# Zeros, x and conversions moved in the opening of a three-layer kernel

## The chip, the cores and the metric

The kernel runs on one core of one Trainium2 chip. Its time is device microseconds (us) of one execution; the kernel before takes 930.06 us (median of 3 runs, 930.0 to 930.53). One execution was also recorded by the profiler: it took 930.29 us, of which 928.4 us lie between its first and its last instruction (the span). In the rows, PE is TensorE, PEld its weight loads, DVE VectorE, ACT ScalarE, POOL GpSimd and SP SyncE, whose queue issues most DMAs.

## The reference

```python
def mab(q, kv):                                   # one attention, scale = 1/sqrt(128)
    s = scale * (q @ kv.transpose(0, 2, 1))
    s = s - s.max(-1, keepdims=True)
    a = np.exp(s)
    a /= a.sum(-1, keepdims=True) + 1e-09
    return a @ kv
h = mab(I, x)                                     # x: 12480 x 128, I: 32 x 128
x = mab(x, h)                                     # 12480 x 128
h = x @ w_in                                      # 128 -> 2048
x = (np.maximum(h, 0) + alpha * np.minimum(h, 0)) @ w_out
h = np.maximum(x @ w2_in, 0)                      # 128 -> 2048
out = (h * h) @ w2_out
```

x and I are 32-bit floats, the four weight matrices 64-bit floats.

## The kernel before, in words

**Opening.** The first attention (32 queries over all 12480 rows of x) goes over seven groups: group 0 has 4 tiles of 48 rows, groups 1 to 6 have 4 tiles of 512. For each group PE transposes x (`transpose_x`, L290), DVE and ACT copy the result into `xT` (L293), PE makes the scores (L302), DVE their running maximum (L318 to L322), ACT the exponentials (L331) and the factor for older sums (L326), PE transposes those (`transpose_e`, L346), ACT copies them (L352), and PE multiplies them with x (`values1`, L360); DVE adds the result into `h_run` (L367). The values of a group are taken in the turn of the next. Loops are in the order written; a tile's readers and writers wait by semaphore, and every engine and every DMA queue works strictly in its order.

**Keeping PE at work.** Ahead of the first x, and between short pieces, PE multiplies a tile of zeros into a bank that nobody reads (`keep_busy`, L97).

**Conversions.** The weights arrive as pairs of 32-bit words (`load_w`, 512 KB a piece, four buffers). A piece is made into 32-bit floats in five steps (`to_f32`): MAG (ACT, L196), LOW (ACT, L199), BITS (DVE, L203), SIGN (DVE, L209), ADD (POOL, L212). `convs[0..3]` are the pieces of w_in, `convs[4..7]` those of w_out, which have three steps more: REST (POOL, L227, times 1 - alpha), HI (ACT, L232, the rounded part) and LO (POOL, L217, what is left). They stand between the attention's steps, where the code puts them. A raw buffer is free for the next load once its ADD is done.

**From the first attention to the layers.** The normalized result is `hT` (L486). From it PE makes the scores of the first tile of 512 rows (L513), `w1h` and `w1l` (hT times w_in, split in two), whose rows SP's DMAs spread into `w1s` (L650). PIECES are the eight pieces of the second MLP's weights.

**Main loop.** Step s does four parts of the MLPs for 128 of 2048 columns of one tile of rows: `l1_a(s)` (one matmul, L729, then ACT L735 and DVE L742 split it in `g1h` and `g1l`), `l1_b` of an earlier step (three matmuls with `wo_hi` and `wo_lo`, L747 to L749), and the same for the second MLP from step 24 on (7 matmuls more). 25 tiles of 16 chunks make 400 steps. Before step 24 `l1_a` writes four banks in turn, so that `l1_a(s)` waits until DVE has read the bank of step s - 4; `l1_b(i)` comes at step i + 5. Work that comes once is put at a step by `at(step, ...)`: it follows that step's matmuls. At step 12 `step_v` (L701) multiplies all 16 chunks of `w_out_sb` in 16 small matmuls, chunk by chunk.

```python
    at(8, scale_wa)
    at(8, second[6])
    at(12, step_v)
```

## Time and profile before

| What | Value |
|---|---|
| Median of 3 runs | 930.06 us |
| The profiled execution | 930.29 us |
| Its span | 928.4 us |
| PE busy | 921.3 us (99%) |
| DVE, ACT, POOL busy | 644.2, 728.7, 535.7 us |
| First x transposed on PE, from | 3.28 us |
| `hT` written, from | 38.06 us |
| First matmul of step 0 | 43.58 us |

The profile tells one execution. The chain of waits is followed back from the last instruction: it names at each moment the engine for which the end waited. The timeline gives instructions in order of time, merged where neighbours are alike; a row's second number runs from the start of the first to the end of the last, so matmuls that overlap are read by the distance of their starts. A matmul of 32-bit floats counts twice in these rows.

### The profile page before, as it was taken

The page shows a single profiled execution, that of the slowest core. Times are in us where ns is not written, and L with a number is a line of the kernel's source. Part 1 is how long each engine was busy: PE and PEld are TensorE (multiplying, and loading weights), DVE is VectorE, ACT ScalarE, POOL GpSimd, SP SyncE. Part 2 cuts the span into 40 slices and gives each one's busy share as a digit, 9 for nine tenths or more (in the row PEclk, how much of TensorE's full clock was granted, in tenths as well). Part 3 has the DMA queues.
Part 4 walks back from the last instruction along what each step waited for, and adds up shares of the span by engine and source line. Part 5 has one row for each costly group of instructions (what it writes and reads, how often), then busy time and mean ns, then how long its engine had stood idle before and what let it go on. Part 6 is the DMA issues. An engine that isn't in the chain of part 4 may idle for free.

```text
span 928.4 us, 13643 instructions
## 1 busy us (share of the span) xinstructions
PE 921.3 (99%) x4549; PEld 784.2 (84%) x4549; DVE 644.2 (69%) x1014; ACT 728.7 (78%) x1336; POOL 535.7 (58%) x436
## 2 busy tenths in 40 slices
PE   9999999999999999999999999999999999999998
PEld 7677888888888888888888888888888888899997
DVE  5898776666666766667766666766666766666677
ACT  6889877777777787777787777877777877878776
POOL 2568755655555665555665555665555565655530
PEclk9999999999999999999999999999999999999999
DMA  9551000010000020000020000020000010000000
GB/s 344 179 151 47 7 7 12 21 37 12 1 12 12 1 57 13 1 12 13 1 57 12 1 12 7 7 57 2 12 12 1 12 36 15 12 12 11 1 11 19
DMA packets 64551, 29.00 MB, mean 31 GB/s; under 512 B 52208, under 2 KB 57440, under 8 KB 64480
## 3 DMA queue, kind: packets, MB, share of 16 engines
q1 hardware_dynamic: 64000, 27.52, 12.0%
q8 instruction: 36, 0.59, 0.3%
q10 hardware_dynamic: 480, 0.61, 0.2%
q14 instruction: 35, 0.29, 0.1%
HBM read 14.80 MB, written 6.39 MB: 23 GB/s over the span
## 4 chain that ended last, share of the span: by engine, by line
PE 93%; DVE 1%; ACT 1%; DMA 0%; issue 0%; SPq 0%; ACTq 0%
PE y L749 18%; PE y L747 18%; PE y L748 18%; PE h L747 9%; PE h L749 9%; PE h L748 9%; PE h L729 9%; DVE g1l L742 1%; PE y L765 1%; PE ms L570 1%; DVE mag L209 0%; ACT g1h L735 0%; DMA w1s<-w1h 0%; PE h L728 0%; PE y L701 0%
## 5 line engine op out<-in xcount | busy, mean ns | idle before, releaser
L792 POOL TENSOR_TENSOR g2l<-sq,g2h 128x512 fp32r<-128x512 f32 (+1 forms) x376 | 477.0, 1269 | 320.1 <-ACT g2h L790 277.4
L742 DVE SCALAR_TENSOR_TENSOR g1l<-h,g1h 128x512 fp32r<-128x512 f32 (+2 forms) x399 | 269.0, 676 | 215.8 <-ACT g1h L735 213.2
L735 ACT ACTIVATE g1h<-h 128x512 fp32r<-128x512 f32 (+2 forms) x400 | 234.1, 588 | 123.6 <-PE h L729 120.8
L783 DVE TENSOR_TENSOR sq<-h,r 128x512 f32<-128x512 f32 (+2 forms) x400 | 271.1, 678 | 44.0 <-ACT r L781 13.7
L781 ACT ACTIVATE r<-h 128x512 f32<-128x512 f32 (+2 forms) x400 | 235.2, 588 | 54.0 <-PE h L749 14.3
L790 ACT CAST g2h<-sq 128x512 fp32r<-128x512 f32 (+2 forms) x400 | 240.9, 602 | 0.4 <-DVE sq L783 0.3
L729 PE MATMUL h<-a_s,w1s 128*128 128x512 f32 (+3 forms) x400 | 151.1, 379 | 1.2 <-DVE g1l L742 0.7
L747 PE MATMUL h<-y1h,w2i_hi 128*128 128x512 f32 (+2 forms) x400 | 151.1, 378 | 0.4 <-DVE sq L783 0.2
L749 PE MATMUL y<-g2l,w2o_hi 128*128 128x512 f32 (+2 forms) x400 | 150.8, 377 | 0.0
L747 PE MATMUL y<-g1h,wo_hi 128*128 128x512 f32 (+2 forms) x400 | 150.6, 377 | 0.0
L749 PE MATMUL h<-y1l,w2i_hi 128*128 128x512 f32 (+2 forms) x400 | 150.6, 377 | 0.0
L749 PE MATMUL y<-g1l,wo_hi 128*128 128x512 f32 (+2 forms) x400 | 150.6, 377 | 0.0
L747 PE MATMUL y<-g2h,w2o_hi 128*128 128x512 f32 (+2 forms) x400 | 150.6, 377 | 0.0
L748 PE MATMUL y<-g2h,w2o_lo 128*128 128x512 f32 (+2 forms) x400 | 150.6, 376 | 0.0
L748 PE MATMUL h<-y1h,w2i_lo 128*128 128x512 f32 (+2 forms) x400 | 150.6, 376 | 0.0
L748 PE MATMUL y<-g1h,wo_lo 128*128 128x512 f32 (+2 forms) x400 | 150.5, 376 | 0.0
L729 PEld LDWEIGHTS h<-a_s,w1s 128*128 128x128 f32 (+1 forms) x400 | 74.9, 187 | 16.4 <-DVE g1l L742 3.0
L747 PEld LDWEIGHTS h<-y1h,w2i_hi 128*128 128x128 f32 x400 | 74.9, 187 | 13.7 <-DVE g1l L742 1.0
L748 PEld LDWEIGHTS y<-g1h,wo_lo 128*128 128x128 f32 x400 | 75.0, 187 | 12.3
L747 PEld LDWEIGHTS y<-g1h,wo_hi 128*128 128x128 f32 x400 | 75.0, 187 | 11.9
L749 PEld LDWEIGHTS y<-g2l,w2o_hi 128*128 128x128 f32 x400 | 74.9, 187 | 11.9 <-DVE g2l L792 0.2
L749 PEld LDWEIGHTS h<-y1l,w2i_hi 128*128 128x128 f32 x400 | 74.9, 187 | 11.5
(160 smaller groups left out, 659.6 us busy)
## 6 DMA issues: line engine op xcount, KB each, us to landing
out_dram<-o SPq DMA_DIRECT2D x84, 64.0 KB, 2.0
xg<-in_x_dram SPq DMA_DIRECT2D x8, 512.0 KB, 9.5
raw<-in_moe_w_in_dram SPq DMA_DIRECT2D x8, 512.0 KB, 5.7
raw<-in_moe_w_out_dram SPq DMA_DIRECT2D x8, 512.0 KB, 5.0
a_s<-a_hi SPq DMA_DIRECT2D x40, 64.0 KB, 2.0
a_s<-a_lo SPq DMA_DIRECT2D x40, 64.0 KB, 2.0
x_last<-in_x_dram SPq DMA_DIRECT2D x2, 512.0 KB, 9.6
out_dram<-o SPq DMA_DIRECT2D x12, 56.0 KB, 1.9
```

Of the source, the lines that this page charges most:

```text
L570: nc.tensor.matmul(b[i * M : (i + 1) * M, :w], hT[:, :M], xT[:, first_token[t + 1] - w : first_token[t + 1]], start=True, stop=True, tile_ ...
L729: nc.tensor.matmul(eights(b[:, :w]), w1s[: a.shape[0], c * P : (c + 1) * P], eights(a), start=True, stop=True)
L735: nc.scalar.activation(hi, b[:, :w], AF.Relu)
L742: nc.vector.scalar_tensor_tensor(lo, b[:, :w], 0.0, f32(hi), op0=ALU.max, op1=ALU.subtract)
L747: nc.tensor.matmul(b, w_hi, hi, start=start, stop=False)
L748: nc.tensor.matmul(b, w_lo, hi, start=False, stop=False)
L749: nc.tensor.matmul(b, w_hi, lo, start=False, stop=stop)
L765: nc.tensor.matmul(eights(b), v_s[: a.shape[0]], eights(a), start=False, stop=True)
L781: nc.scalar.activation(r, b, AF.Relu)
L783: nc.vector.tensor_tensor(sq, b, r, op=ALU.mult)
L790: nc.scalar.copy(hi, sq)
L792: (nc.vector if i >= total - LAG2 else nc.gpsimd).tensor_tensor(lo, sq, f32(hi), op=ALU.subtract)
```

## The change

Five zero matmuls stand at the beginning in place of four, and the transposition of the inducing rows (`indT`) comes right behind them, ahead of the first x. In the loop over groups, the values of the group before are no longer behind the scores but between the transposition of the next x and the next scores, half on either side of `transpose_e`; the ACT copy of a group's first tile stands ahead of its exponentials. BITS, SIGN and ADD of a piece of w_in come one group after its MAG and LOW. The pieces of w_out follow by one place each: where `convs[5]` and `convs[6]` were handled, `convs[4]` and `convs[5]` are, and the end of `convs[6]` and all of `convs[7]` but its load stand in steps 4 to 13 of the main loop. x of groups 2 and 3 is loaded whole ahead of the piece of w_in beside it, x of group 6 ahead of the first w_out, and PIECES[2] and PIECES[3] are loaded at steps 5 and 10.

```diff
--- before.py
+++ after.py
@@ -96,7 +96,7 @@
         for _ in range(n):
             nc.tensor.matmul(b[:, :P], v, v, start=True, stop=True)
 
-    keep_busy(4, idle_bank)
+    keep_busy(5, idle_bank)
 
 
 
@@ -234,7 +234,7 @@
         def low():
             pool_lo(lo, a, hi)
 
-        return to_f32("w_out", k, lambda: f, h2_bank if k == 2 else None) + [rest, high, low]
+        return to_f32("w_out", k, lambda: f, h2_bank if k == 1 else None) + [rest, high, low]
 
     def conv_w2(name, k, tags, bank):
         f = []
@@ -266,12 +266,10 @@
     al_raw = st.tile([NCH, P], F32, name="al_raw", tag="al_raw")
     load_x(0)
     load_x(1)
-    load_x(2, 0)
+    load_x(2)
     load_w("w_in", 0)
-    load_x(2, 1)
-    load_x(3, 0)
+    load_x(3)
     load_w("w_in", 1)
-    load_x(3, 1)
     nc.sync.dma_start(out=al_raw, in_=alpha.rearrange("(c p) -> c p", p=P))
     load_x(4)
     load_w("w_in", 2)
@@ -373,48 +371,52 @@
             v()
 
     convs = [conv_w_in(k) for k in range(4)] + [conv_w_out(k) for k in range(4)]
-    evac = transpose_x(0)
-    run(evac)
+    MAG, LOW, BITS, SIGN, ADD, REST, HI, LO = range(8)
+
     indT = keep_tile("indT", [P, M])
     b = free_bank()
     nc.tensor.transpose(b[:, :M], ind, ident[:M, :M])
     nc.vector.tensor_copy(indT, b[:, :M])
+    evac = transpose_x(0)
+    run(evac)
     idle_bank = y2_bank()
     keep_busy(1, idle_bank)
+    b = scores(0)
+    keep_busy(1, idle_bank)
     for g in range(last - 1):
+        maxima(g, b)
+        evac = transpose_x(g + 1)
+        if g > 1:
+            values1(g - 1, range(2))
+        elif g:
+            values1(0)
+        evac[0]()
+        exps(g, b)
+        run(evac[1:3])
+        if g:
+            factor(g)
+        evac[3]()
+        transpose_e(g)
+        copy_e(g)
+        if g > 1:
+            convs[g - 2][BITS]()
+            values1(g - 1, range(2, TILE1[2]))
+            convs[g - 2][SIGN]()
+            convs[g - 2][ADD]()
+            if g == 2:
+                load_x(last)
+            load_w("w_out", g - 2)
+        sums(g)
         if g:
             run(convs[g - 1][:2])
-        b = scores(g)
-        if g:
-            values1(g - 1)
-        else:
-            keep_busy(1, idle_bank)
-        maxima(g, b)
-        exps(g, b)
-        if g:
-            factor(g)
             add_values(g - 1)
-            convs[g - 1][2]()
-        run(transpose_x(g + 1))
-        transpose_e(g)
-        copy_e(g)
-        sums(g)
-        if g:
-            run(convs[g - 1][3:5])
-        if 1 < g and g + XBUFS - 1 <= last:
-            load_x(g + XBUFS - 1)
-        if 0 < g <= 4:
-            load_w("w_out", g - 1)
         if g == 2:
             b = y2_bank()
             nc.tensor.transpose(b[:, :NCH], al_raw, ident[:NCH, :NCH])
             nc.vector.tensor_copy(al, b[:, :NCH])
             nc.vector.tensor_scalar(al1, al, -1.0, 1.0, op0=ALU.mult, op1=ALU.add)
-
-    MAG, LOW, BITS, SIGN, ADD, REST, HI, LO = range(8)
-
-    b = scores(last - 1)
-    convs[4][MAG]()
+        b = scores(g + 1)
+
     evac = transpose_x(last)
     maxima(last - 1, b)
     evac[0]()
@@ -425,15 +427,12 @@
     factor(last - 1)
     transpose_e(last - 1)
     copy_e(last - 1)
-    convs[4][LOW]()
-    convs[4][BITS]()
-    convs[4][SIGN]()
-    convs[4][ADD]()
+    run(convs[4][:2])
+    run(convs[3][BITS : ADD + 1])
+    load_w("w_out", 3)
     sums(last - 1)
     b = scores(last)
     values1(last - 2)
-    convs[4][REST]()
-    convs[5][MAG]()
     maxima(last, b)
     exps(last, b)
     factor(last)
@@ -452,8 +451,8 @@
     values1(last - 1, range(2, 4))
     b = ms_bank()
     nc.tensor.matmul(b[:, :1], m_rep.rearrange("o q j -> o (q j)"), ones[:1, :], start=True, stop=True)
-    convs[5][BITS]()
-    convs[5][SIGN]()
+    convs[4][BITS]()
+    convs[4][SIGN]()
     add_values(last - 1)
     sums(last)
     wgt = att.tile([P, 1], F32, name="wgt", tag="wgt")
@@ -461,12 +460,11 @@
     sel = st.tile([P, P], F32, name="sel", tag="sel")
     nc.scalar.mul(sel, same, wgt)
     values1(last)
-    convs[5][LOW]()
-    convs[5][ADD]()
-    convs[6][MAG]()
-    convs[6][LOW]()
+    convs[4][ADD]()
+    convs[4][REST]()
+    run(convs[5][:2])
+    run(convs[6][:2])
     convs[4][HI]()
-    run(convs[7][:2])
     idle_bank = h1_bank()
 
     d = ms_bank()
@@ -487,12 +485,11 @@
         hT.rearrange("c (q j) -> c q j", q=Q), b[:, :P].rearrange("c (q j) -> c q j", q=Q),
         den.unsqueeze(1).to_broadcast([P, Q, M]), op=ALU.mult,
     )
-    convs[6][BITS]()
-    convs[6][SIGN]()
+    convs[5][BITS]()
+    convs[5][SIGN]()
+    convs[5][ADD]()
     convs[5][REST]()
     convs[4][LO]()
-    convs[6][ADD]()
-    convs[6][REST]()
 
 
     a_s = {}
@@ -677,18 +674,15 @@
     first_w1s_low(0, P)
     first[5]()
     first_w1s_low(P, 512)
+    copy_w1f()
     convs[5][HI]()
-    convs[6][HI]()
-    copy_w1f()
     load_w(*PIECES[0][:2])
     load_w(*PIECES[1][:2])
     for v, k in (("hi", 1), ("lo", 1), ("hi", 2), ("lo", 2)):
         spread_w1s(v, k)
-    load_w(*PIECES[2][:2])
     spread_w1s("hi", 3)
     spread_w1s("lo", 3)
     convs[5][LO]()
-    convs[6][LO]()
     run(second[:2])
 
 
@@ -841,18 +835,27 @@
 
     at(1, second[2])
     at(3, step_wa)
-    at(4, convs[7][BITS])
-    at(4, convs[7][SIGN])
-    at(4, convs[7][ADD])
+    at(4, convs[6][BITS])
+    at(4, convs[6][SIGN])
+    at(4, convs[6][ADD])
     at(5, second[3])
     at(5, second[4])
-    at(6, load_w, *PIECES[3][:2])
+    at(5, load_w, *PIECES[2][:2])
+    at(6, convs[7][MAG])
+    at(6, convs[7][LOW])
     at(7, second[5])
-    at(7, convs[7][REST])
+    at(7, convs[6][REST])
     at(8, scale_wa)
     at(8, second[6])
-    at(11, convs[7][HI])
-    at(11, convs[7][LO])
+    at(9, convs[7][BITS])
+    at(9, convs[7][SIGN])
+    at(9, convs[7][ADD])
+    at(10, load_w, *PIECES[3][:2])
+    at(10, convs[6][HI])
+    at(10, convs[6][LO])
+    at(11, convs[7][REST])
+    at(13, convs[7][HI])
+    at(13, convs[7][LO])
     at(12, step_v)
     at(14, copy_v)
     at(16, split_v)
```

How the order on the engines moves, at two places; the names are those of the tiles written and read.

PE before, from the transposed exponentials of group 1 (`e` into `y`) to the scores of group 3 (`ms`); L290 transposes x of group 3, L360 are the values of group 1, L410 transposes alpha:

```order
L346 MATMUL y_261<-ident,e 128x128 x4
L302 MATMUL ms<-xT,indT 32x512 x4
L360 MATMUL y_281<-xg,eT 32x128 x16
L290 MATMUL h_309<-ident,xg 128x128 x4
L290 MATMUL h_314<-ident,xg 128x128 x4
L290 MATMUL h_319<-ident,xg 128x128 x4
L290 MATMUL h_324<-ident,xg 128x128 x4
L346 MATMUL y_333<-ident,e 128x128 x4
L410 MATMUL y_348<-ident,al_raw 128x16
L302 MATMUL ms<-xT,indT 32x512 x4
```

PE after the change, over the same stretch (lines L344, L300, L288, L358 and L415 are the former L346, L302, L290, L360 and L410):

```order
L344 MATMUL y_257<-ident,e 128x128 x4
L300 MATMUL ms<-xT,indT 32x512 x4
L288 MATMUL h_278<-ident,xg 128x128 x4
L288 MATMUL h_283<-ident,xg 128x128 x4
L288 MATMUL h_288<-ident,xg 128x128 x4
L288 MATMUL h_293<-ident,xg 128x128 x4
L358 MATMUL y_298<-xg,eT 32x128 x8
L344 MATMUL y_316<-ident,e 128x128 x4
L358 MATMUL y_298<-xg,eT 32x128 x8
L415 MATMUL y_344<-ident,al_raw 128x16
L300 MATMUL ms<-xT,indT 32x512 x4
```

The values moved behind the transposition of x, half of them ahead of the transposed exponentials and half behind.

DVE before, in steps 7 to 11 of the main loop: the low parts `g1l` of steps 7 to 11, with the transposition for the second attention (`a2t`) and the scaling `wa` between them:

```order
L742 SCALAR_TENSOR_TENSOR g1l<-h_816,g1h 128x512
L600 STREAM_TRANSPOSE a2t<-a_740 128x512
L742 SCALAR_TENSOR_TENSOR g1l<-h_828,g1h 128x512
L661 TENSOR_TENSOR wa<-y_775,al 128x512
L742 SCALAR_TENSOR_TENSOR g1l<-h_863,g1h 128x512
L742 SCALAR_TENSOR_TENSOR g1l<-h_872,g1h 128x512
L742 SCALAR_TENSOR_TENSOR g1l<-h_881,g1h 128x512
```

DVE after the change, over the same steps (`mag` is the last piece of w_out):

```order
L736 SCALAR_TENSOR_TENSOR g1l<-h_809,g1h 128x512
L597 STREAM_TRANSPOSE a2t<-a_730 128x512
L736 SCALAR_TENSOR_TENSOR g1l<-h_821,g1h 128x512
L658 TENSOR_TENSOR wa<-y_765,al 128x512
L736 SCALAR_TENSOR_TENSOR g1l<-h_856,g1h 128x512
L203 TENSOR_SCALAR mag<-mag 128x512
L209 SCALAR_TENSOR_TENSOR mag<-raw,mag 128x512
L736 SCALAR_TENSOR_TENSOR g1l<-h_868,g1h 128x512
L736 SCALAR_TENSOR_TENSOR g1l<-h_881,g1h 128x512
```

BITS and SIGN of a second piece came in behind the low part of step 9.

POOL before, from the low part of step 1 to the first piece of the second MLP (`wf`):

```order
L217 TENSOR_TENSOR g1l<-wf,g1h 128x512
L585 TENSOR_TENSOR a_740<-a_740,mx 128x512
L212 TENSOR_TENSOR w_out_sb<-mag,raw 128x512
L596 TENSOR_TENSOR a_740<-a_740,sm 128x512
L227 TENSOR_TENSOR aw<-w_out_sb,al_118 128x512
L217 TENSOR_TENSOR a_lo<-a2t,a_hi 128x512
L217 TENSOR_TENSOR wo_lo<-aw,wo_hi 128x512
L212 TENSOR_TENSOR wf<-mag,raw 128x512
```

POOL after the change, over the same stretch:

```order
L217 TENSOR_TENSOR g1l<-wf,g1h 128x512
L582 TENSOR_TENSOR a_730<-a_730,mx 128x512
L212 TENSOR_TENSOR w_out_sb<-mag,raw 128x512
L593 TENSOR_TENSOR a_730<-a_730,sm 128x512
L227 TENSOR_TENSOR aw<-w_out_sb,al_119 128x512
L217 TENSOR_TENSOR a_lo<-a2t,a_hi 128x512
L212 TENSOR_TENSOR w_out_sb<-mag,raw 128x512
L217 TENSOR_TENSOR wo_lo<-aw,wo_hi 128x512
L227 TENSOR_TENSOR aw<-w_out_sb,al_119 128x512
L217 TENSOR_TENSOR wo_lo<-aw,wo_hi 128x512
L212 TENSOR_TENSOR wf<-mag,raw 128x512
```

The first `w_out_sb` row was `convs[7]` and is `convs[6]`; the ADD and REST of `convs[7]` and the LO of `convs[6]` now stand behind `a_lo`, and the ADD is ahead of that LO.

## Rows read from the trace of the kernel before

**Rows 1.** The page: busy us (share of the span) xinstructions; shares of the chain of waits.

```profile
PE 921.3 (99%) x4549; PEld 784.2 (84%) x4549; DVE 644.2 (69%) x1014; ACT 728.7 (78%) x1336; POOL 535.7 (58%) x436
...
PE 93%; DVE 1%; ACT 1%; DMA 0%; issue 0%; SPq 0%; ACTq 0%
```

**Rows 2.** Stretches: us, busy us (count) of each engine, granted clock, DMA share, GB/s.

```profile
10.00:20.00 10.00, 10.00 (x125) 7.43 (x123) 7.38 (x19) 8.14 (x19) 1.99 (x2) 1.00 1.05 397
...
60.00:84.00 24.00, 23.49 (x102) 17.12 (x102) 21.98 (x36) 23.25 (x46) 18.52 (x15) 1.00 0.38 110
84.00:900.00 816.00, 816.00 (x3788) 702.38 (x3788) 554.02 (x830) 642.10 (x1155) 489.89 (x388) 1.00 0.08 14
```

**Rows 3.** Timeline of PE at the start: start us, us, instruction, xcount [idle before <-releaser].

```profile
1.05 2.07 PE L97 MATMUL ms<-zeros 128*128 128x128 f32 x8 [1.05 <-DVE ones L114]
3.28 0.63 PE L290 MATMUL h<-ident,x 48*128 48x48 f32 x4 [0.15 <-POOL same L109]
...
5.71 3.62 PE L290 MATMUL h<-ident,xg 128*128 128x128 f32 x16
...
9.47 1.72 PE L302 MATMUL ms<-xT,indT 128*32 128x512 f32 x8
```

**Rows 4.** Timeline of PE over groups 2 to 5.

```profile
13.86 1.38 PE L302 MATMUL ms<-xT,indT 128*32 128x512 f32 x8
...
18.57 1.15 PE L302 MATMUL ms<-xT,indT 128*32 128x512 f32 x8
19.46 1.14 PE L360 MATMUL y<-xg,eT 128*32 128x128 f32 x32
20.53 1.97 PE L290 MATMUL h<-ident,xg 128*128 128x128 f32 x16
...
22.90 1.31 PE L302 MATMUL ms<-xT,indT 128*32 128x512 f32 x8
...
27.40 1.31 PE L302 MATMUL ms<-xT,indT 128*32 128x512 f32 x8
28.64 1.97 PE L290 MATMUL h<-ident,xg 128*128 128x128 f32 x16
```

**Rows 5.** DMA issues from 17.05 us: last half of x; KB, us to landing.

```profile
xg<-in_x_dram SPq DMA_DIRECT2D x1, 512.0 KB, 10.7
```

**Rows 6.** Timeline of DVE, and of ACT, between hT and step 0.

```profile
39.05 0.69 DVE L209 SCALAR_TENSOR_TENSOR mag<-raw,h 128x512 int32<-128x512 int32 x1
...
42.66 1.35 ACT L232 CAST wo_hi<-aw 128x512 fp32r<-128x512 f32 x2
```

**Rows 7.** Timeline of DVE, steps 2 to 13.

```profile
46.49 1.89 DVE L742 SCALAR_TENSOR_TENSOR g1l<-h,g1h 128x512 fp32r<-128x512 f32 x3 [0.18 <-ACT g1h L735]
48.30 0.42 DVE L203 TENSOR_SCALAR mag<-mag 128x512 int32<-128x512 int32 x1
48.75 0.69 DVE L209 SCALAR_TENSOR_TENSOR mag<-raw,mag 128x512 int32<-128x512 int32 x1
...
54.27 2.67 DVE L742 SCALAR_TENSOR_TENSOR g1l<-h,g1h 128x512 fp32r<-128x512 f32 x4
57.30 0.69 DVE L742 SCALAR_TENSOR_TENSOR g1l<-h,g1h 128x512 fp32r<-128x512 f32 x1 [0.36 <-ACT g1h L735]
```

**Rows 8.** Timeline of POOL, steps 4 to 11.

```profile
49.52 1.31 POOL L212 TENSOR_TENSOR w_out_sb<-mag,raw 128x512 int32<-128x512 int32 x1 [1.18 <-DVE mag L209]
...
55.80 1.29 POOL L217 TENSOR_TENSOR wo_lo<-aw,wo_hi 128x512 fp32r<-128x512 f32 x1 [0.68 <-ACT wo_hi L232]
```

**Rows 9.** Timeline of PE, steps 10 to 13.

```profile
51.75 0.51 PE L729 MATMUL h<-a_s,w1s 96*128 96x512 f32 x1 [0.46 <-DVE g1l L742]
...
54.81 1.08 PE L701 MATMUL y<-w_out_sb,wa 128*32 128x128 f32 x32
55.83 0.49 PE L729 MATMUL h<-a_s,w1s 96*128 96x512 f32 x1
```

**Rows 10.** DMA issues: rows of w1 at 41.23 and at 48.14 us.

```profile
w1s<-w1h SPq DMA_DIRECT2D x2, 64.0 KB, 2.0
...
w1s<-w1l SPq DMA_DIRECT2D x2, 64.0 KB, 4.9
```

## The prediction

> **What bounds the kernel now.** Read the page first. PE is busy for 921.3 of 928.4 us, and the chain of waits runs over PE for 93% of the span [rows 1]. The stretches show where that is strict: from 84 to 900 us PE stands still for nothing [rows 2]. The change touches no instruction that runs there, so it is worth what it does to the moment at which that stretch begins, and every microsecond by which PE is late then is paid in full. The part ahead of it has three regimes, read from the timelines. Up to about 28 us the groups of the first attention follow each other on PE, each as long as its own matmuls plus what the last copy of x costs. From there to step 0 at 43.58 us one chain runs through maxima, sums, hT and the first softmax over several engines. In steps 0 to 9 DVE sets the pace (at 51.75 PE waits 0.46 us for a low part of DVE [rows 9]), and from 51.75 us on PE is dense again up to 66 us. DVE has caught up by 57.30, where it idles 0.36 us for want of work [rows 7]: whatever PE loses at steps 12 and 13, no backlog gives back.
>
> **Start (fifth zero, indT first).** The eight rows of four zero matmuls take 2.07 us from 1.05 [rows 3], so a fifth adds 0.4 to 0.5 and ends near 3.4; indT takes some 0.1, and x of group 0 starts near 3.5 where it started at 3.28. What was behind it shrinks: indT no longer stands between x and the scores. I put the first transposition of group 1 at 5.35 us for 5.71 [rows 3]: -0.35 us, bounds 0 and -0.5.
>
> **The clock.** [...] PE had worked with short pauses since 1.05 us, and the rise came within the scores at 9.47 us, whose 1.72 us fall to 1.15 in group 3. If fewer pauses ahead bring the rise forward into the transpositions of group 1, half of them (half of 3.62 - 1.97, 0.8 us) and the scores (1.72 - 1.15, 0.6) become cheap. No row shows when it will come. Bounds: 0 (no earlier) and -2.2 (all of both). I take -1.3, near the half.
>
> [...]
>
> **x ahead of w_in.** Group 6's last half of x landed at 17.05 + 10.7 = 27.75 us [rows 5], and PE began on that group at 28.64 [rows 4], on that half some 0.9 later: x is early by 1.8 us. The change takes one 512 KB piece (w_out) from ahead of it, 1.3 us at the 397 GB/s of the full DMA stretch [rows 2], so PE may be 3.1 us earlier there before x is late; by the terms here it is 2.35 earlier. I cost the DMA order at nothing, since the groups before hide it; without the 1.3 it would cost 0.55 us.
>
> **Groups.** Scores of groups 2 to 5 start at 13.86 and 27.40: 13.54 us for three turns, 4.51 each [rows 4]. The cheapest is 18.57 to 22.90, 4.33. In the others the fourth score matmul waits for ACT's copy of the fourth tile. With the values in between (1.07 us from 19.46 to 20.53) that copy has time. The other loop, scores to maximum to exponential to its transposition, keeps the transposition of x (1.97) ahead of its end and gets half the values (0.5) beside it, so nothing new should wait there. ACT's and DVE's conversions are one piece per group as before. I take 4.28 a turn: 3 x (4.51 - 4.28) = -0.7 us (0 to -1.2), and -0.15 for the turn to group 6 (group 5's scores take 1.31 us with that wait, group 3's 1.15).
>
> **From group 6 to step 9.** PE's and DVE's chain through hT is as long as before: where `convs[6]` stood between hT and the first maximum, `convs[5]` now stands, with the same 0.69 us SIGN from a bank [rows 6]. What becomes free is ACT ahead of step 0: one HI instead of two (1.35 us for two [rows 6]) frees ACT 0.68 us earlier for the first `g1h`, from which DVE's chain through steps 0 to 9 starts; DVE's own work ahead of its first low part uses up the rest. I take half, -0.35 us (0 to -0.68). On SP, PIECES[1] now waits for an ADD that POOL ends at about 41.07 (SIGN ends at 39.74, plus 1.31) where it had long been issued, and the rows of w1 stand behind it in SP's queue: 0.2 us later. Their data also queue behind 512 KB. Step 4 is the first to need them. Its low part is the third of the three from 46.49 us, at 47.7 [rows 7], now 47.35. A low part starts 1.47 us after its matmul when DVE stands idle for it (55.83 to 57.30 for step 13 [rows 7, 9]), so the rows may land until 45.9 us. I cost this at nothing; the third rival prices it.
>
> **Step 12.** This is the part that costs. `step_v` reads every chunk of `w_out_sb`, and its last quarter is `convs[7]`. Before, that ADD ended at 50.83 us [rows 8], 4 us ahead of `step_v` at 54.81 [rows 9]. Now BITS and SIGN stand on DVE behind the low part of step 9. In the clock of before: that low part starts at 54.27, and the next of the four stands 0.66 behind it ((2.67 - 0.69)/3); BITS and SIGN take 1.14, from 48.30 to the end of the SIGN at 49.44 [rows 7], and so end at 56.07; ADD starts 0.08 later and takes 1.31 [rows 8]: 57.46. `step_v` would reach its last quarter at 54.81 + 3/4 of 1.02 = 55.58. PE stands still for 1.9 us, and everything behind it in PE's queue with it. LOW and MAG of this piece on ACT at step 6 fall into ACT's wait for `a2t` and cost nothing. Next late is the LO of `convs[6]`, which now stands behind that ADD on POOL: 57.46 + 1.29 = 58.75 [rows 8], while `l1_b(8)` asks for it with its second matmul, some 0.55 behind step 13's first row at 55.83 + 1.9, at 58.3: 0.45 us more. REST, HI and LO of `convs[7]` follow within 3 us; their reader, `l1_b(12)`, comes four steps later. BITS and SIGN themselves (1.1 us of DVE) hide in PE's standstill. Sum +2.35 us; bounds +1.3 (if the pieces start a full matmul step earlier) and +3.2 (if the HI behind it blocks ACT for its whole wait).
>
> **The sum.** -0.35 - 1.3 - 0.7 - 0.15 - 0.35 + 2.35 = -0.5 us on the profiled execution's 930.29, of which 928.4 is span and the rest does not change: 929.8. That execution lies 0.23 us above the median of the runs, so the median to expect is 930.06 - 0.5 = 929.5 us.
>
> **Rivals.**
> First, the clock rises no earlier. For it: before, the zeros were nearly as dense and did not bring it; against: two pauses of a few tenths go. All else equal, +1.3: 930.9 us.
>
> Second, the standstill at step 12 is given back. PE has waits of its own between 60 and 84 us, where ACT is busy 23.25 and DVE 21.98 of 24 us [rows 2]: 0.51 us of idle time, and by the distances of its matmuls, which overlap in the rows, an estimated 1.7 in sum. If these come from a backlog that a pause at step 12 would clear, the sum falls to 927.8. Against it: DVE's idle 0.36 us at 57.30 [rows 7] says that there is no backlog at that point.
>
> Third, the rows of w1 come late, and the kernel gets slower. Behind a 512 KB piece they took 4.9 us to land where they take 2.0 [rows 10]. Issued from 41.45 us on, in place of 41.23, the last that step 4 reads (some 1.2 later) would land at 47.5. It decides from 45.9 us on, as above; at 47.5 DVE's chain is 1.6 us late: 931.1 us, slower than before. Against it: in the row quoted another piece was moving too, and PIECES[1] is issued 5 us earlier than that one was.
>
> [...]
>
> **Chances.** Forecast 0.42, first rival 0.28, second 0.16, third 0.14. The first two differ by too little to be told apart by the time alone. A measurement of this kernel can tell about 0.2%, 1.86 us, from no change: faster means under 928.2, slower over 931.9. The forecast and the first rival lie within that band but for a tenth at either end; the second lies below it for the most part; the third above it only with the clock low as well (932.4). That gives faster 0.19, same 0.69, slower 0.12. The range leaves one tenth out on each side: from the second rival, 927.9, to midway between the third alone and both, 931.7.
>
> **What would show it.** In the timeline of PE after the change: 16 transpositions of group 1 in under 3 us (clock), turns of 4.3 us between scores of groups 2 to 5, the first row of step 0 at about 41.1 us, then a wait inside `step_v` for POOL's `w_out_sb` of 1.9 us, and one for `wo_lo` right after. The forecast is wrong if PE shows no wait at `step_v`, if step 0 comes later than 42.5, or if step 4 waits for DMAs.

## The result, and the profile after

The changed kernel takes 935.06 us (median of 6 runs, 934.50 to 935.41) where the kernel before takes 930.03 (6 runs, 929.92 to 930.53): ratio 1.0051, 95% interval 1.0041 to 1.0061. It is slower by 5.0 us. The prediction was 929.5, with a range from 927.9 to 931.7 and a chance of 0.12 for slower.

The page after, with the same lines as [rows 1]: span, busy time of each engine, the chain of waits by engine.

```profile
span 933.6 us, 13649 instructions
...
PE 923.5 (99%) x4551; PEld 784.1 (84%) x4551; DVE 645.6 (69%) x1014; ACT 728.7 (78%) x1336; POOL 535.4 (57%) x436
...
PE 91%; ACT 0%; DVE 0%; issue 0%
```

PE is busy 2.2 us longer with only two instructions more (the fifth zeros). The stretches say where: us, busy us (count) of each engine, granted clock, DMA share, GB/s.

```profile
57.00:60.00 3.00, 1.23 (x11) 0.59 (x12) 2.02 (x4) 1.26 (x3) 2.70 (x3) 1.00 0.40 94
60.00:63.40 3.40, 3.40 (x9) 2.66 (x10) 1.52 (x3) 2.19 (x6) 2.10 (x2) 0.50 0.46 110
63.40:84.00 20.60, 20.23 (x86) 15.26 (x85) 18.21 (x30) 19.09 (x38) 13.34 (x11) 1.00 0.48 142
84.00:900.00 816.00, 816.00 (x3787) 700.87 (x3786) 555.39 (x832) 644.00 (x1159) 493.88 (x392) 1.00 0.08 14
```

After 3.00 us of which PE is busy for 1.23 come 3.4 us with a granted clock of 0.50, in which PE is always busy and does about half as much: 9 matmuls, 2.6 a us, where the stretch from 84 us on has 4.6 a us. From 84 to 900 us PE is dense, as in [rows 2]. So the loss lies ahead of 64 us. The starts of the same instructions in the two profiled executions:

| starts at (us) | before | after | later by |
|---|---|---|---|
| scores of group 2 | 13.86 | 13.90 | 0.04 |
| scores of group 5 | 27.40 | 27.97 | 0.57 |
| scores of group 6 | 31.33 | 31.64 | 0.31 |
| hT on DVE | 38.06 | 38.56 | 0.50 |
| step 0 | 43.58 | 44.08 | 0.50 |
| step 4 | 45.78 | 47.64 | 1.86 |
| step 10 | 51.75 | 52.85 | 1.10 |
| step 13 | 55.83 | 58.99 | 3.16 |
| step 16 | 58.68 | 63.84 | 5.16 |
| step 31 | 84.04 | 89.22 | 5.18 |

Four places, then: the groups and hT (0.5), the way to step 10 (0.6), `step_v` between steps 10 and 13 (2.1), and steps 13 to 16 (2.0). Nothing is given back behind.

**The opening.** PE's timeline, columns as in [rows 3].

```profile
1.05 2.50 PE L97 MATMUL ms<-zeros 128*128 128x128 f32 x10 [1.05 <-DVE ones L114]
3.66 0.28 PE L378 MATMUL ms<-ident,ind 32*128 32x32 f32 x1
3.88 0.66 PE L288 MATMUL h<-ident,x 48*128 48x48 f32 x4
...
6.10 3.23 PE L288 MATMUL h<-ident,xg 128*128 128x128 f32 x16
...
9.36 1.68 PE L300 MATMUL ms<-xT,indT 128*32 128x512 f32 x8
```

x starts 0.60 us later than in [rows 3] and the transpositions of group 1 0.39 later; they end at 9.33 in both all the same, since the trace's clock records give the full clock from 8.78 us on, where before they give it from 10.33 (a stretch ahead of the first record prints 1.00, as 5.60 to 9.00 us does in the trace before, so that only the rows tell the clock there). At the scores of group 2, 0.04 later, the two have cancelled.

**A turn of the groups.** PE's timeline, group 3, to be held against [rows 4].

```profile
18.79 1.06 PE L300 MATMUL ms<-xT,indT 128*32 128x512 f32 x8
19.78 1.96 PE L288 MATMUL h<-ident,xg 128*128 128x128 f32 x16
21.68 0.64 PE L358 MATMUL y<-xg,eT 128*32 128x128 f32 x16
22.25 0.74 PE L344 MATMUL y<-ident,e 128*128 128x128 f32 x4
22.93 0.65 PE L358 MATMUL y<-xg,eT 128*32 128x128 f32 x16
23.39 1.04 PE L300 MATMUL ms<-xT,indT 128*32 128x512 f32 x8
```

No bracket, so PE waits for nothing, and yet the turn lasts 4.60 us. Start to start: scores 0.99, transpositions of x 1.90, half the values 0.57, transpositions of e 0.68, the other half 0.46. Before, the turn from 18.57 took 4.33 with the same matmuls: scores 0.89, values 1.07, both transpositions 2.37 (here 2.58). What differs is the order. The new one has four passages a turn between matmuls of the form `128*32` (scores, values) and those of `128*128` (transpositions), where the old has two: by an estimate from these two turns, 0.27 us over two further passages, 0.13 us each. That the length goes with the order, two of the experiments below show, one from either side; what a passage costs by itself is not shown.

**hT.** DVE, then POOL, at the last sum.

```profile
36.33 0.98 DVE L333 SCALAR_TENSOR_TENSOR s_run<-s_run,f,s_g 128x1 f32<-128x1 f32 x1
...
38.56 0.29 DVE L484 TENSOR_TENSOR hT<-y,den 128x128 f32<-128x128 f32 x1
```
```profile
35.99 1.30 POOL L212 TENSOR_TENSOR w_out_sb<-mag,raw 128x512 int32<-128x512 int32 x1 [2.13 <-issue]
```

One element a partition took 0.98 us, until POOL's addition ended at 37.29. Before, nothing ran on POOL beside this sum, and the same kind of wait stood further up, at a SIGN beside POOL's REST (34.43 to 35.72):

```profile
34.85 1.41 DVE L209 SCALAR_TENSOR_TENSOR mag<-raw,mag 128x512 int32<-128x512 int32 x1
...
36.45 0.20 DVE L335 SCALAR_TENSOR_TENSOR s_run<-s_run,f,s_g 128x1 f32<-128x1 f32 x1
```

There PE had work until 36.93, the end of the values; here the sum is what the next matmul waits for.

**Step 4.** PE, then SP.

```profile
47.64 0.70 PE L723 MATMUL h<-a_s,w1s 96*128 96x512 f32 x2 [1.58 <-DVE g1l L736]
```
```profile
37.32 4.71 SPq L182 DMA_DIRECT2D raw<-in_moe_w_in_dram  x2
42.12 1.22 SPq L647 DMA_DIRECT2D w1s<-w1h  x2
```

The second load of that pair is PIECES[1]; SP waits for POOL with it until about 42, and the rows of w1 go out behind it, 0.9 us later than in [rows 10] (0.5 of it because hT is later), with 512 KB ahead of them. The last rows that step 4 reads were issued at 43.39 and took 4.1 us, to 47.5; before, issued at 42.55, they took 1.9. The piece ahead of them, issued at 41.68, landed at 46.88, and the first of the rows, issued at 42.12, 0.2 us behind it, at 47.08. The bracket names DVE, whose low part ended at 47.50 as well; the first experiment tells the two apart.

**Steps 12 to 16.** PE.

```profile
55.95 0.86 PE L695 MATMUL y<-w_out_sb,wa 128*32 128x128 f32 x24
58.63 0.43 PE L695 MATMUL y<-w_out_sb,wa 128*32 128x128 f32 x8 [1.83 <-POOL w_out_sb L212]
58.99 0.50 PE L723 MATMUL h<-a_s,w1s 96*128 96x512 f32 x1
59.32 0.41 PE L741 MATMUL y<-g1h,wo_hi 128*128 128x512 f32 x1
59.87 0.71 PE L742 MATMUL y<-g1h,wo_lo 128*128 128x512 f32 x1
60.38 0.63 PE L743 MATMUL y<-g1l,wo_hi 128*128 128x512 f32 x1
60.80 0.63 PE L723 MATMUL h<-a_s,w1s 96*128 96x512 f32 x1
```

The wait of 1.83 us in `step_v` is the one predicted (1.9), and the matmul with `wo_lo` stands some 0.3 behind its neighbour as well. Then matmuls start 0.43 us apart where they stood 0.23 apart in steps 10 to 12: the halved clock, 0.50 from 59.98 to 63.40 us by the clock records.

### The profile page after: what moved, and what is told of

It reads as the page before. It is cut to its first block, busy times and chain, and to the rows that moved or that the text cites. A ratio compares the mean times of both kernels' runs of the same rounds, so it can differ in the third digit from the quotient of the medians.

```text
span 933.6 us, 13649 instructions
## 1 busy us (share of the span) xinstructions
PE 923.5 (99%) x4551; PEld 784.1 (84%) x4551; DVE 645.6 (69%) x1014; ACT 728.7 (78%) x1336; POOL 535.4 (57%) x436
## 4 chain that ended last, share of the span: by engine, by line
PE 91%; ACT 0%; DVE 0%; issue 0%
PE y L743 18%; PE y L741 18%; PE y L742 18%; PE h L741 9%; PE h L743 9%; PE h L742 9%; PE h L723 9%; PE y L759 1%; PE ms L567 1%; PE h L722 0%; ACT g1h L729 0%; ACT r L775 0%; DVE mag L209 0%; DVE g1l L736 0%; ACT ms L196 0%
## 5 line engine op out<-in xcount | busy, mean ns | idle before, releaser
L743 PEld LDWEIGHTS y<-g1l,wo_hi 128*128 128x128 f32 x400 | 75.3, 188 | 11.6
```

Of the source, the lines that this page charges most:

```text
L743: nc.tensor.matmul(b, w_hi, lo, start=False, stop=stop)
```

## The experiments

The theory after reading the trace: the standstill in `step_v` also halves the clock, the rows of w1 are late, and the opening gains nothing. All times are medians; the kernel before took 930.02 to 930.25 beside them.

**PIECES[1] behind the rows of w1**, on the changed kernel:

```diff
-    load_w(*PIECES[1][:2])
     for v, k in (("hi", 1), ("lo", 1), ("hi", 2), ("lo", 2)):
         spread_w1s(v, k)
     spread_w1s("hi", 3)
     spread_w1s("lo", 3)
+    load_w(*PIECES[1][:2])
```

> The load of PIECES[1] stands behind the rows of w1 in SP's queue instead of ahead of them; nothing else differs from the changed kernel (935.06 us). Theory (the rows of w1 are held up by that load, in SP's queue and in the DMA rings): the first matmul of step 4 no longer waits (PE stood idle 1.58 us ahead of it), it begins about 1.3 us behind the w1f transpositions at most, and step 10 comes 0.9 us earlier; the standstill at step 12 keeps its length, so the time falls by 0.9 us to about 934.1. Rival (the wait at step 4 is covered, since DVE sets the pace of steps 0 to 9 anyway): 935.0, step 10 unmoved.

933.88 us (5 runs), ratio 1.0037 (1.0025 to 1.0049). The wait is gone from step 4, which had 1.58 us of it:

```profile
44.71 1.54 PE L723 MATMUL h<-a_s,w1s 96*128 96x512 f32 x4 [0.27 <-DVE a_s L553]
46.09 0.60 PE L654 MATMUL y<-ident,w1f 128*128 128x128 f32 x4
46.77 0.75 PE L723 MATMUL h<-a_s,w1s 96*128 96x512 f32 x2
```

From step 0 to step 10 it takes 7.99 us (after 8.77, before 8.17). So the late rows cost 0.8 us; in the median 1.2 are gained, and part of that is that the mean granted clock stayed at 0.999 or 1.000 in four of its five executions, where it was 0.998 in all six of the changed kernel. The profiled one is the fifth: there the clock halves from 58.69 us on, behind a wait in `step_v` of 1.84 us.

**Work for PE in the wait**, on the changed kernel, ahead of `step_v`'s last quarter:

```diff
         for c in range(NCH):
             q = c % Q
+            if c == 12:
+                keep_busy(8, ms_bank(), ident)
```

> Eight multiplications of the identity with itself, into a bank nobody reads, stand ahead of chunk 12 of step_v, so that PE works through its wait for the last ADD; the wait itself stays. Theory (the standstills at steps 12 and 13 bring TensorE's clock down, and the low clock costs some 1.7 us by itself): the granted clock stays 1.00 in the stretch 58 to 64 us, the matmuls of steps 14 and 15 stand 0.23 us apart instead of 0.43, and the time falls by 1.7 us to about 933.4. Rival (the clock falls for another reason, or its fall is hidden behind the low parts of DVE): clock and time as in the changed kernel, 935.0, or up to 0.2 more for the added work.

934.30 us (6 runs), ratio 1.0043 (1.0031 to 1.0055), which is less than the theory asked. In one of the six executions the mean clock was still 0.997 (935.08 us). The profile is plainer: the granted clock is 1.00 throughout, and from step 13 to 16 it takes 3.25 us instead of 4.85, though step 13 comes at the same 58.9.

```profile
56.60 2.05 PE L97 MATMUL ms<-ident 128*128 128x128 f32 x16
58.58 0.42 PE L697 MATMUL y<-w_out_sb,wa 128*32 128x128 f32 x8
58.94 0.50 PE L725 MATMUL h<-a_s,w1s 96*128 96x512 f32 x1
```

**`step_v` without its last quarter**, on the changed kernel:

```diff
-                v_bank[0][q * M : (q + 1) * M, :P], w1["wa scaled"][:, q, c // Q], w_out_sb[:, c, :],
+                v_bank[0][q * M : (q + 1) * M, :P], w1["wa scaled"][:, q, c // Q], w_out_sb[:, min(c, c % 4 + 8), :],
```

> step_v reads chunks 8 to 11 a second time in place of chunks 12 to 15 (so the second MLP's input is not the reference's): it no longer needs the last ADD. Theory (POOL's order is the bound: LO of convs[6] stands behind that ADD, and l1_b(8) needs it right after step_v): the wait leaves step_v and comes back at l1_b(8), 2.0 to 2.3 us long, the clock falls as before, and the time stays at 934.9 +- 0.3. Rival (step_v's wait alone is the cost): the time falls by 1.9 us to 933.2, or by 3.6 to 931.4 if the clock stays up as well.

934.86 us (5 runs), ratio 1.0047 (1.0034 to 1.0060), as expected. The wait only moves to the low part of `convs[6]`, which stands behind the same addition on POOL, and the clock is halved from 60.06 us on as before:

```profile
55.82 1.08 PE L695 MATMUL y<-w_out_sb,wa 128*32 128x128 f32 x32
59.72 0.52 PE L742 MATMUL y<-g1h,wo_lo 128*128 128x512 f32 x1 [2.15 <-POOL wo_lo L217]
```

**Values behind the scores again**, on the changed kernel (its conversions stay a group later):

```diff
         b = scores(g)
         if g:
             values1(g - 1)
...
-        if g > 1:
-            values1(g - 1, range(2))
-        elif g:
-            values1(0)
```

> In the loop over groups the values stand behind the scores again, the exponentials ahead of the copies, as in the kernel before; conversions, loads and the main loop as in the changed kernel. Theory (PE is dense in the loop, and each change between kinds of matmul costs it about 0.1 us that overlapped before): scores of groups 2 to 5 are 13.5 us apart instead of 14.07, step 0 begins 0.5 us earlier, 934.5 us. Rival (the turns are long for another reason, such as the clock or x): no change, 935.0; if the new order had saved the copy's wait as I forecast, 935.7.

935.91 us (5 runs), ratio 1.0055 (1.0043 to 1.0067): all three numbers missed. Three turns take 14.23 us, not 13.5. The time is near that of the last rival (935.7), but DVE shows another reason, between groups 3 and 4:

```profile
19.87 1.23 DVE L410 TENSOR_SCALAR al<-al 128x16 f32<-128x16 f32 x1
21.02 0.68 DVE L316 TENSOR_REDUCE top<-ms 128x1 f32<-128x512 f32 x1
```

A 16-column operation (0.18 us before) ends with POOL's addition, which ran from 19.77 to 21.07, and the maximum of group 3 comes 1.1 us late. Where nothing is late, the old order is as quick as before: the turn from group 2's scores takes 4.72 us, where the kernel before takes 4.71 and the changed one 4.89. The old order does not go with conversions in the new places.

**The conversions back**: the kernel before with the start, the order of the loads and the order of the groups changed, the conversions in their old places.

```diff
-    keep_busy(4, idle_bank)
+    keep_busy(5, idle_bank)
...
-            values1(g - 1)
+        if g > 1:
+            values1(g - 1, range(2))
```

> The kernel before with three of the change's parts: the fifth zeros with indT first, x loaded ahead of w_in, the values in two halves between the transpositions and the scores. The conversions stay in the places of before, PIECES[1] and the steps from 4 on too. Theory: all of the loss comes from the conversions that stand a group (or some steps) later: they bring the late rows of w1 at step 4, the standstill at step 12, the late low part behind it and the halved clock, and the POOL addition that holds DVE up in the chain to hT. Then this kernel is at 929.5 to 930.5 us, step 0 at 43.3 to 43.9 us, step 13 at 55.5 to 56.2. First rival: the order of the groups costs by itself what the trace of after shows in its turns (14.07 us for three, 13.54 before): 930.6 to 931.0. Second rival: the prediction's terms for start, clock and groups hold here without what the conversions undo: 927.8.

931.82 us (11 runs), ratio 1.0022 (1.0013 to 1.0031). hT comes at 39.71, 1.65 later than before, more than either rival said, and the theory is missed (three turns take 14.35 us, the last 4.25). In the first turn ACT waits for a load of w_in. In the third and the last the conversions push DVE's maxima back: the update of the running maximum ends with POOL's addition, here from 30.06 to 31.36, and takes 0.74 us in place of 0.16.

```profile
30.64 0.74 DVE L318 SCALAR_TENSOR_TENSOR nm<-top,nm 128x1 f32<-128x1 f32 x1
```

The turn from 19.41 to 24.02, in which PE waits for nothing, takes 4.61 us, as in the changed kernel, with the conversions of before: the length of the turn goes with the order on PE. From hT on nothing is lost: step 31 stands 1.68 later, and the clock stays full. So what happens behind hT in the changed kernel, 4.7 of its 5.2 us, belongs to the conversions and the loads that follow them.

**Only the last piece of w_out late**, on the kernel before:

```diff
-    at(4, convs[7][BITS])
-    at(4, convs[7][SIGN])
-    at(4, convs[7][ADD])
+    at(9, convs[7][BITS])
+    at(9, convs[7][SIGN])
+    at(9, convs[7][ADD])
```

REST moves from 7 to 11, HI and LO from 11 to 13.

> The kernel before with one edit: the last piece of w_out (BITS, SIGN, ADD) is converted at step 9 where it stood at step 4, its REST at 11, HI and LO at 13; step_v stays at step 12. All loads and all of the first attention as before. Theory (a standstill costs its length and then halves TensorE's clock for a few us): step_v waits 1.5 to 2 us, DVE gains 0.5 ahead of step 10, and the halved clock after it adds some 1.7: 932.7 to 933.3, with a granted clock of 0.5 from about 59 us on. Rival (the prediction's price, the standstill alone): 931.0 to 931.6 and the clock full.

934.71 us (5 runs), ratio 1.0055 (1.0043 to 1.0068), more than the theory; two of the five, the profiled one among them, hold 2.3 us that come later (see the last section). The wait in `step_v` is 1.80 us and the clock falls at 56.67; but step 16 then waits again, 0.93 us, and it is SP that shows why: the load of PIECES[3] still stands at step 6, and it now waits for the same addition ahead of the results of the second attention.

```profile
56.60 0.34 SPq L182 DMA_DIRECT2D raw<-in_moe_w_in_dram  x1
57.05 1.14 SPq L611 DMA_DIRECT2D a_s<-a_hi  x2
```

**The start alone** (five zeros, `indT` first), on the kernel before:

```diff
-    keep_busy(4, idle_bank)
+    keep_busy(5, idle_bank)
...
+    indT = keep_tile("indT", [P, M])
...
     evac = transpose_x(0)
```

> The kernel before with one edit: five zeros ahead of the first x in place of four, and indT before the transpositions of group 0. Theory (x starts 0.6 us later because the zeros are longer and indT's copy goes first, and the earlier clock gives that back): scores of group 2 at 13.8 to 14.0, 929.8 to 930.3 us. The prediction's terms for the start and the clock (-0.35 and -1.3): 928.4. Rival: the later start is not given back, since the clock's rise moves from one execution to the next whatever stands there: 930.5.

930.57 us (11 runs), ratio 1.0004 (0.9995 to 1.0012): no gain. x starts at 3.87 and the clock rises only at 10.95 here. Over all profiles, the rise lies at 7.42 to 10.33 us with the old start (nine executions, median 8.88) and at 8.78 to 10.95 with the new one (seven, median 9.89). It differs by 2 us or more between executions of one and the same opening, and the zeros do not bring it forward. In seven of the nine with the old start it falls among the 16 transpositions of group 1.

Nor is an early rise worth much with the old start. Over those nine executions the scores of group 2 start between 12.83 us (rise at 7.42) and 13.86 (at 10.33), but hT comes between 37.75 and 38.38, and before, with the latest rise of all, at 38.06. In the eight with an earlier rise MAG of the third piece of w_in waits 1.0 to 1.6 us for its load on ACT, and the exponentials of group 3 stand behind it. One of them, with a rise at 8.26 (the last piece at step 7, HI and LO at 14, the load at 10):

```profile
20.13 0.68 ACT L196 ACTIVATE mag<-raw 128x512 f32<-128x512 f32 x1 [1.57 <-DMA raw<-in_moe_w_in_dram]
```

Before, the same MAG starts at 19.29, 0.1 us after the copy ahead of it. In the changed kernel it comes at 23.57 and waits for no load: in the four executions with its whole opening hT comes at 38.56 and 38.59 for a rise at 8.78 and 8.86, and at 39.04 and 39.19 for one at 10.61 and 10.91.

**x ahead of w_in alone**, on the kernel before (`load_x(2)` and `load_x(3)` whole):

```diff
-    load_x(2, 0)
+    load_x(2)
     load_w("w_in", 0)
```

> The kernel before with one edit: x of groups 2 and 3 loaded whole, each ahead of the piece of w_in that stood between its halves. Theory (x lands 1.8 us ahead of its use before, and w_in is not needed before the conversions): no change, 929.8 to 930.3 us. Rival: the conversions of w_in wait for it and hold DVE up in groups 1 and 2: 930.5 to 931.

930.16 us (12 runs), ratio 1.0004 (0.9996 to 1.0013): nothing, as predicted.

**The last piece at step 7**, on the kernel before: BITS, SIGN, ADD at 7, REST at 9, HI and LO at 12; then HI and LO at 14; then the load of PIECES[3] at step 10 as well.

```diff
-    at(6, load_w, *PIECES[3][:2])
+    at(10, load_w, *PIECES[3][:2])
```

> The kernel before with one edit: the last piece of w_out is converted at step 7 (BITS, SIGN, ADD) where it stood at step 4, REST at 9, HI and LO at 12, so that its addition should end just ahead of step_v's last quarter. Theory (DVE sets the pace of steps 4 to 9, and 1.14 us of it moves behind the low part of step 7, PE dense from step 10 on): step 10 starts 0.3 to 0.6 earlier, no wait in step_v: 929.4 to 929.7. Rival: DVE's work is only moved within the stretch that it paces, step 10 is where it was: 930.0. Second rival: ADD is late by some tenths for step_v: 930.5.

> The kernel with the last piece of w_out at step 7 (REST at 9), with its HI and LO at step 14 where they stood at 12. In the run with them at 12, HI stood ahead of the Relus of steps 13 to 15 on ScalarE's queue and waited 1.8 us for its REST, and TensorE lost 1.9 us ahead of step 16. Theory: that wait goes, step 16 starts at 58.3 to 58.8 and the 0.3 to 0.6 us of step 10 are kept: 929.4 to 929.9. Rival: the wait moves on, since LO then comes too late for step 17's second matmul of the second layer: 930.5 to 931.5.

> The kernel with the last piece of w_out at step 7 and its HI and LO at 14, with the next load of w2 (PIECES[3]) at step 10 where it stood at step 6. In the two runs with the load at 6 it waited on SyncE's queue for this piece's addition, ahead of the DMAs that bring the second attention's results (a_s), and TensorE waited 1.3 to 1.5 us for those at step 16. Theory: the load behind them, that wait goes, step 16 starts at 58.6 to 59.2: 930.0 to 930.5. Rival: the results come late all the same, since a_lo stands behind the addition on GpSimd: 931.0 to 932.0.

931.83 (11 runs), 931.99 (10) and 930.65 us (11; ratio 1.0003, 0.9994 to 1.0012). Moving HI did nothing: ScalarE's queue was not what step 16 waited for. Moving the load took 1.3 us away and the wait ahead of step 16 with it (step 16 at 58.96). Step 10 is 0.6 to 0.7 earlier than before in all three and step 12 is 0.1 to 0.2 later: DVE's 1.1 us only change their place. None of them beats the kernel before.

**The clock priced by itself.** First the late piece with the load still at 6, and 14 matmuls in the wait:

> The kernel with the last piece of w_out converted late (its one edit as in that run), and 14 transposing-size matmuls into a spare bank put ahead of step_v's last quarter, so that TensorE works (1.5 us of it) while it waits there for the addition. Theory (in the run with the late piece the halved clock is what makes steps 13 to 16 longer: 5.27 us from step 13 to 16 where the kernel before takes 2.85): the clock stays full, steps 13 to 16 take 3.0 to 3.5 us, and the median is 1.5 to 2 us below that run's, 932.7 to 933.2. Rival (ScalarE's queue, blocked by the HI that waits for its REST, sets these steps, and the clock is only beside it): the clock stays full and the time is within 0.5 us of 934.7, or steps 13 to 16 take over 4.5 us.

933.95 us (5 runs). They took 3.4 us where 1.5 was expected (each is two rows), so step 13 came 1.2 later than without them; the clock stayed full and steps 13 to 16 took 3.71 instead of 5.27 us. The limit of 3.5 was missed because of the wait for `a_s` (0.69). The pair with the load at step 10 has neither fault; the second has seven matmuls:

> The kernel with the last piece of w_out converted at step 9 (the late one), with the load of PIECES[3] at step 10 where it stood at step 6, so that it no longer holds up the DMAs of a_s. Theory: the standstill in step_v (1.8 us idle, 1.4 us net of what DVE gains ahead) stays, and the halved clock behind it adds 1.5 to 1.7: step 13 at 57.1 to 57.3, step 16 at 61.5 to 61.9, 932.8 to 933.3. Rival (the wait for a_s was most of it, the clock little): 931.4 to 932.0.

> The same as the run with the late piece and the load behind, and seven 128-column matmuls into a spare bank ahead of step_v's last quarter, some 1.5 us of work for TensorE inside its wait. Theory: the clock stays full, step 13 at 57.1 to 57.4, step 16 at 60.0 to 60.5, 931.4 to 931.8, that is 1.3 to 1.7 below the same kernel without them. Rival: within 0.5 us of it.

932.43 (11 runs, ratio 1.0020, 1.0011 to 1.0029) and 931.60 us (11 runs, ratio 1.0018, 1.0008 to 1.0027). PE in `step_v` without, then with the matmuls, and the stretch from step 13 to step 16, columns as in [rows 2]:

```profile
56.94 0.60 PE L701 MATMUL y<-w_out_sb,wa 128*32 128x128 f32 x8 [1.81 <-POOL w_out_sb L212]
57.47 0.80 PE L729 MATMUL h<-a_s,w1s 96*128 96x512 f32 x1
...
57.40:61.70 4.30, 4.30 (x17) 3.45 (x14) 1.69 (x3) 2.89 (x6) 1.89 (x2) 0.64 0.45 106
```
```profile
54.54 1.83 PE L97 MATMUL ms<-ident 128*128 128x128 f32 x14
56.45 0.42 PE L703 MATMUL y<-w_out_sb,wa 128*32 128x128 f32 x8
...
56.80:59.70 2.90, 2.90 (x17) 2.39 (x14) 0.81 (x3) 2.31 (x6) 1.84 (x2) 1.00 0.41 97
```

The same 17 matmuls, 4.30 us at a mean granted clock of 0.64 and 2.90 at 1.00. In seven of the eleven executions of the first the mean clock over the span is 0.997 or 0.998, and those take 932.3 to 933.3 us; in four it is 1.000, and those take 931.6 to 932.0. With the matmuls it is never under 0.999, and yet the medians differ by 0.8 only and the ratios overlap, less than the 1.3 to 1.7 expected: four of the eleven without them kept the clock, and three of the eleven with them took 933.7 to 934.2 at the full clock. So the price rests on the stretch (1.4 us) and on the two kinds of execution of the first kernel (1.1 between their medians): a standstill of 1.8 us in this place halves the clock in most executions but not in all, and that costs 1.1 to 1.4 us. It did so in all six of the changed kernel and in all five with the load at step 6, but in one of five with PIECES[1] behind the rows of w1, whose profile has the same standstill; what decides it is not shown.

## Why the prediction was wrong

The sum was -0.5 us on the profiled execution and came out at +5.1. By its own terms:

- *Start*, -0.35, came out at +0.39 for the transpositions of group 1: x starts at 3.88 where 3.5 was forecast, since the zeros and indT's row end later than allowed, and taking indT from behind x won 0.21 us where the term counts on 0.57.
- *The clock*, -1.3: the step failed. It took the time at which the clock rises for an effect of the pauses ahead. The profiles show a time that wanders by over 2 us under the same instructions. In this pair of executions the rise happened to be 1.55 earlier and just paid for the later start; that is luck, and over the profiles the first rival was right (median 9.89 with the new start, 8.88 with the old). No run shows the 1.3: the 16 transpositions of group 1 became 0.39 us shorter and the scores behind them 0.04. Nor did the term ask what an earlier rise meets: with the old start ACT's wait for w_in takes most of it away.
- *x ahead of w_in*, 0: right.
- *Groups*, -0.7 and -0.15, came out at +0.53 (14.07 us for three turns) and -0.26 (3.67 for 3.93). The argument looked for waits and removed one of 0.2 us. It took for the new turn less than the cheapest turn of before, without adding up PE's own rows in the new order, which come to 4.6. The two further passages could have been counted, and part of what they may cost stood in the same trace: at group 6, where halves of the values alternate with a transposition already, the half at 33.77 and the transposition at 34.36 take 0.59 and 0.68 us from start to start, where half of the values in [rows 4] takes 0.53 and the transposition of e behind them 0.57 (22.33 to 22.90).
- *From group 6 to step 9*, -0.35: hT to step 0 takes 5.52 us in both. Behind it the first `g1h` starts 0.55 us after step 0 where it started 0.82 after, and DVE's first low part 1.32 for 1.45; where the rows of w1 are not late (the first experiment) step 4 is 0.14 and step 10 0.18 earlier. So the freed HI gave half of its term, and in the changed kernel the rows of w1 hide it. hT itself lost 0.2 to the addition on POOL that now stands beside the last sum; the prediction called this chain as long as before and did not ask what POOL does beside it. The sum took 0.98 us in place of 0.20 and ended with POOL's addition of 1.30; why is not shown.
- *The rows of w1*, 0: the third rival's price was the truth in kind. It had the rows that step 4 reads land at 47.5, where they did (issued 0.7 us later and 0.8 quicker than it said), and put DVE's chain at 1.6 late; step 4 was 1.4 later relative to step 0, and 0.6 to 0.8 of it were left at step 10.
- *Step 12*, +2.35, came out at +4.06: the standstill (1.83 for 1.9) and the late low part (0.3 for 0.45) were right, and the claim that no backlog gives it back too. What is missing is the halved clock behind it, 1.6 us by the pair in the profiles of the changed kernel, with and without work in the wait.

So of the 5.6 us between sum and result, 1.7 are start and clock, 1.1 the groups, 0.5 hT and the freed HI, 0.6 the rows of w1 (0.4 and 0.8, if what HI gave is counted), and 1.7 step 12. The sign of the whole was set at step 12, where a wait of known length was priced at its length.

Open: what the new order of the groups would be worth with its conversions placed so that DVE never meets POOL. The three variants run (14.07, 14.23, 14.35 us for three turns) were each late for a reason of their own. The 13.54 of before is a strict measure: in eight other executions with the old start and order, where the turns begin earlier and wait for w_in, they take 13.63 to 14.25. What holds against the order is the turn in which PE waits for nothing, 4.60 us for 4.33.

## What to carry to other kernels

A standstill of the matmul engine can cost more than its length (here 1.1 to 1.4 us on top of 1.8): see what the clock does behind it, and if the wait can't go, fill it with matmuls that nobody needs, but measured ones, since too many are a wait themselves (3.4 us of them in a wait of 1.8 put the next step 1.2 later). When an instruction is moved later, follow each queue in which it now stands in front of something: here POOL's low part, SP's rows of w1 and, in one experiment, SP's results of another stage. A gain at the head of a pipeline is worth what the next wait leaves of it: the early clock rises with the old start ended at a wait of 1.0 to 1.6 us for a load. And before a gain is booked for a new order, add up the busy engine's own rows in that order.

## What was not expected of the hardware

- The clock falls after 1.8 us of standstill in some executions and not in others (7 of 11 in one kernel), and its rise at the start wanders from 7.4 to 11.0 us over the sixteen profiled executions.
- Matmuls of 512 columns start mostly 0.22 to 0.24 us apart in steps 17 to 30, most often 0.230, and 0.220 apart from step 31 on (84.04 us before, 89.22 after), with the granted clock at 1.00 in all of these. In two of the sixteen profiled executions (of the kernel with x ahead of w_in, and of the one with the piece at 9 and the load at 6) the 0.230 lasts to 134 us, which costs them 2.3 us. Other executions stand some 2.3 us above the rest at the full clock (three of 27 of the kernel before, 932.3 to 932.7) and may be of this kind. No run was made to find why; the moments compared above lie ahead of it.
- Four VectorE operations of one or sixteen columns took 0.63 to 1.23 us in place of 0.16 to 0.20 and ended with an addition on GpSimd (19.23 and 36.33 us after the change, 19.87 with the values behind the scores, 30.64 with the conversions back); a copy of sixteen columns beside the first of these additions took 0.17, as before.
